# A searched schedule re-drawn, and three more buffers for the last output tiles: pooled attention into a gated conv FFN

## The chip, the cores and the metric

The kernel runs on one core of a Trainium2 chip. The metric is device time of one execution in microseconds, the median of three runs. Engines are called as in the profile: PE (TensorE matmul), PEld (its weight load), DVE (VectorE), ACT (ScalarE), POOL (GpSimd), SP (SyncE). POOL, SP and ACT issue DMAs.

## What is computed

Eight batches, eight heads, 576 positions, head size 64; all inputs and the output are float32.

```python
k_p = k.reshape(B, H, 72, 8, D).mean(axis=3)      # 72 pooled keys per head
v_p = v.reshape(B, H, 72, 8, D).mean(axis=3)
attn = softmax(scale * q @ k_p.T)                 # 576 x 72 for each head
x = (attn @ v_p), heads side by side              # (8, 576, 512)
h = maximum(x @ w_in, 0)                          # 512 -> 1024
conv_out = 3-tap convolution of h along the positions, conv_w per feature
out = (h * sigmoid(conv_out)) @ w_out             # 1024 -> 512, (8, 576, 512)
```

## The kernel before

**Tiles and stages.** Batches are taken in four groups of two. A group's attention runs in tiles of 128 rows of positions, nine to a group (ten in group 0). For a batch k, q and v are loaded (as bf16, by casting DMAs on POOL's queue; batch 0's k and q come as float32 over SP's queue into the two buffers `hT`, and are cast by ACT and DVE at L307). Keys are pooled on PE with a pooling matrix (L432, L442), or by adds on DVE (`pool_pair`, L465, group 1 on); the pooled keys are cast to `kT` (L457), queries are turned into `qT` (L542 on PE, copy at L560), values are pooled on DVE (L512, L516). An attention tile takes scores on PE (L608), the maximum on DVE (`negm`, L634), the exponential on ACT, a transpose with a copy `eT` (L707), the product with the values (L718), a reciprocal (L731), the scaling (L739 on ACT or L746 on DVE), and a turn of x into `xT` (for the early groups L763 on PE with the copy L771; later by DMA, L755).

**The FFN.** It runs by batch, in eight blocks of 128 features: `ffn_in` (L776, PE) and the relu (L785, ACT) into `hT`. The convolution of the early batches runs on PE (`ffn_conv`, L940). For batches 4 to 7 and half of batch 3 it runs on DVE, with two instructions a block (`ffn_tap`, L912), into one of three accumulators `tg`. Positions are laid out so that a tap is a shift by 64 columns; the first and last 64 columns need copies from the other end, and these are the **wraps**: `ffn_wrap` makes two small copies (L860, L861) for two feature blocks at a time, on POOL or on ACT. The outermost columns are zero, set once by `clear_ends` (four POOL memsets, L855 and L856). After the second tap ACT takes the sigmoid or tanh (L922) into `gT`, and DVE multiplies four blocks by h (`ffn_times`, L990). With all gates of a batch, or of both batches of the group for the tiles of the second, the output projection runs (`ffn_out`, L998, PE, eight matmuls a tile), then a copy to SBUF (`ffn_copy`, L1009, DVE or ACT) and two stores of 64 rows (L1021, queue of SP or ACT).

**Buffers.** `rings` (L218) says how many buffers of each kind there are. Output tiles use the ring `osb` (five), but the nine of group 3 use a ring of their own, `late`: eight halves of the four `qp` buffers, which held queries and are free by then.

**The order.** All instructions belong to ops that the builder puts into a graph. Nothing plans at run time: the class `Graph` holds tables that a search has written. An entry n of ORDER emits op n // 2 on engine n % 2 of those that it may run on; -1 emits a spare matmul (`fill`, L425) that keeps PE busy. FORMS says which matmul tiling an op takes where it may choose, PLACES which buffer of its ring each tile gets. Each engine then runs its own part of that list in order, waiting on semaphores for the others.

```python
for n in self.ORDER:
    o = spares.pop(0) if n < 0 else self.ops[n // 2]
    o.engine = list(o.engines)[0 if n < 0 else n % 2]
```

`clear_ends` is bound by one edge, `ends = add({"POOL": 0.8}, 0, clear_ends, after=raws)` (L1114): it comes after the casts of batch 0's raw keys and queries, which lie in the same buffers. POOL's loads share one DMA queue.

Of the kernel before, what the change touches and what calls it, by code (L numbers as in the profile page):

```python
# [33 lines left out]
class Graph:  # L34
# [38 lines left out]
        0, 16, 4, 24, 12, 44, 28, 8, 10, 14, 32, -1, -1, 42, 36, -1, -1, 40, -1, -1,  # L73
        2, -1, 38, -1, 66, 64, -1, -1, 19, 68, -1, 48, 21, -1, 60, -1, -1, 46, 102, 7,
        26, 34, 114, 118, 106, 116, 121, 108, 104, 113, 111, 122, 126, 125, 292, 128, -1, 74, 30, 294,
        358, -1, -1, 70, 360, 296, -1, -1, 298, 50, 362, 364, 336, 338, 58, 314, 300, 316, 340, -1,
        -1, 342, 130, -1, 318, -1, 344, 320, 132, 380, 303, 134, 322, 382, 347, 194, 196, 136, 384, 201,
        324, 72, 348, 386, 326, 199, 350, 366, 352, 78, 304, 369, 328, 206, 306, 330, 202, 209, 308, 370,
        204, 388, 354, 391, 372, -1, 548, 374, 310, 332, 550, 313, 392, 357, 394, 552, 396, 526, 554, 376,
        528, 398, 335, 570, 556, 401, 572, 530, 226, 532, 558, 574, 379, 228, 230, 576, 504, 444, 506, 84,  # L80
        233, 446, 62, 138, 508, 448, 482, 438, 510, 140, 440, 142, 426, 56, 442, 534, 428, 484, 432, 430,
        144, 434, 537, 52, 486, 76, 512, 488, 420, 436, 422, 514, 80, 560, 54, 424, 516, 402, 562, 518,
        564, 414, 416, 520, 404, 418, 466, 406, 210, 472, 470, 468, 212, 578, 566, 474, 408, 568, 476, 410,
        580, 478, 238, 412, 456, 241, 480, -1, 458, 450, 460, 214, 538, 452, 522, 540, 454, 542, 234, 525,
        462, -1, -1, 237, 582, 216, 262, 221, 584, 464, 82, 225, -1, -1, 219, -1, 223, -1, -1, 265,
        978, 586, 544, 490, 980, 547, 770, 588, 592, 982, 591, 493, 772, 748, 984, 594, 750, 600, 774, 597,
        752, 776, 258, 146, 494, 261, 602, 496, 148, 498, 1000, 605, 934, 608, 1002, 754, 150, 500, 1004, 778,
        503, 610, 936, 781, 756, 152, 613, 624, 759, 154, 626, 614, 86, 1006, -1, 938, 760, 642, 628, 156,
        90, 644, 940, 762, 158, 956, 764, 646, 1008, 942, 958, 94, 1011, 704, 630, 945, 706, 98, 632, 960,
        636, 22, 634, 638, 708, 672, 640, 160, 962, 242, 1012, 96, 676, -1, 782, 674, 986, 1014, 784, -1,  # L90
        88, 1016, 989, 792, 766, 794, 710, 654, 656, 786, 769, 1018, 796, 658, 964, 990, 967, 244, 946, 660,
        1021, 992, 948, 994, 662, 798, 968, 950, 664, 788, 800, 970, 791, 246, 678, 972, 803, 162, 248, 680,
        804, 682, 164, 92, 974, 255, 806, 666, 808, 257, 253, 668, 251, 166, 977, 810, 168, 1186, -1, 670,
        952, 1188, 100, 996, 813, -1, -1, 1190, 999, 694, 955, 170, 1204, 696, 1096, 1206, 1098, 698, 172, 726,
        1192, 1060, 1208, 1100, 1062, 728, 712, 1064, 648, 174, 730, 715, 650, 1090, 176, 652, 1092, 684, 732, 1168,
        688, 1094, 1170, 1104, 1072, 690, 1074, 178, 692, 270, 1076, 1172, 716, 273, 1066, 700, 1194, 1068, 1174, 616,
        1070, 718, 1176, 686, 618, 721, 1084, 180, -1, 702, 1086, 621, -1, 1088, 1150, 1140, 1152, 1210, 1078, 1118,
        1142, 1212, 1080, 1144, 1124, 266, 1082, 1154, 1054, 606, 269, 1102, 1056, 1120, 1196, 1058, 622, 734, 1126, 1428,
        737, 1222, 1198, 830, 1430, 1156, 290, 1224, 1201, 814, 1432, 816, 1226, 1128, 1178, 274, 738, 1122, 832, 819,
        740, 182, 722, 1180, 820, 838, 742, 725, 1182, 835, 744, 840, 1106, 747, 1184, 276, 1410, 843, 1134, 1412,  # L100
        1228, 1158, 884, 1136, 1108, 886, 1138, 1112, 1214, 1230, 888, 878, 1216, 1110, 1414, 880, 1446, 1218, 882, 872,
        1448, 874, 1434, 1220, 918, 278, 876, 1450, 890, 288, 922, 1146, 892, 920, 1160, 894, 846, 1162, 1114, 1165,
        860, 1148, 866, 1436, 868, 1116, 862, 184, 1166, 870, 848, 1130, 864, 280, 1132, 851, 1232, 1202, 283, 284,
        1234, 908, 287, 1236, 1676, 186, 1238, 910, 854, 912, 1678, 1438, 856, 1452, 1440, 836, 1680, 896, 858, 898,
        1442, 1416, 1454, 1640, 188, 902, 900, 1642, 1316, 190, 906, 1644, 1418, 1318, 904, 192, 1392, 1320, 924, 1394,
        1444, 1646, 1322, 1396, 928, 1324, 926, 914, 1280, 1326, 1456, 1398, 1282, 1334, 1458, 930, 1292, 1461, 1400, 1286,
        1288, 1382, 1294, 1648, 1284, 1304, 916, 1296, 1306, 1290, 1462, 1298, 1308, 932, 1300, 1328, 1682, 1402, 1310, 844,
        1302, 1404, 1384, 1312, 1407, 1330, 822, 1336, 1684, 824, 1342, 1314, 1408, 1338, 1604, 827, 1332, 1658, 1420, 1660,
        1340, 1046, 598, 1422, 1606, 1425, 1048, 1662, 1256, 1608, 1664, 1426, 1650, 1376, 1051, 1896, 1842, 1652, 1610, 1258,
        1898, 852, 1655, 1844, 1264, 1900, 1612, 1266, 1846, 1386, 1344, 1261, 1878, 1686, 1666, 1902, 1880, 1269, 1538, 1688,  # L110
        1882, 1848, 1540, 828, 1622, 1378, 1542, 1520, 1624, 1522, 1380, 1656, 1532, 1690, 1524, 1534, 1626, 1346, 1526, 1692,
        1348, 1528, 1536, 1860, 1364, 1530, 1550, 1614, 1262, 1022, 1628, 1616, 1350, 1619, 1548, 1668, 1630, 1862, 1030, 1670,
        1354, 1032, 1352, 1270, 1864, 1673, 1496, 1366, 1498, 1052, 1502, 1356, 1504, 1368, 1584, 1904, 1024, 1358, 1370, 1500,
        1508, 1586, 1674, 1510, 1506, 1632, 1027, 1372, 1544, 1514, 1866, 1634, 1516, 1620, 1360, 1374, 1038, 1590, 1518, 1040,
        1637, 1388, 1272, 1362, 1884, 1274, 1638, 1512, 1578, 1240, 1035, 1546, 1390, 1850, 1588, 1906, 1242, 1580, 1036, 1480,
        1592, 1043, 1482, 1277, 1908, 1596, 1868, 1582, 1746, 1910, 1594, 1748, 1598, 1044, 1752, 1750, 1754, 1570, 1600, 1734,
        1564, 1756, 1736, 1485, 1740, 1552, 1784, 1245, 1742, 1566, 1246, 1248, 1744, 1554, 1568, 1852, 1572, 1488, 1912, 1738,
        1854, 1782, 1602, 1574, 1758, 1760, 1886, 1556, 1870, 1558, 1857, 1250, 1028, 1802, 1490, 1560, 1762, 1764, 1858, 1872,
        1493, 1796, 1766, 1562, 1888, 1874, 1472, 1768, 1890, 1876, 1798, 1893, 1786, 1776, 1808, 1778, 1474, 1804, 1253, 1894,
        1464, 1576, 1477, 1806, 1770, 1478, 1810, 1800, 1772, 1466, 1816, 1774, 1494, 1780, 1988, 1790, 1812, 1946, 1818, 1486,  # L120
        1952, 1789, 1954, 1822, 1820, 1948, 1278, 1792, 1956, 1710, 1950, 1824, 1990, 1794, 1254, 1994, 1834, 1976, 1826, 1982,
        1828, 1469, 1978, 1836, 1992, 1712, 1980, 1830, 1984, 2008, 1970, 1832, 1718, 1814, 1838, 1964, 1986, 1966, 2010, 2001,
        1958, 1840, 1972, 1720, 1974, 2040, 1715, 1960, 2046, 1922, 1716, 1962, 2042, 1999, 1924, 2012, 1470, 2048, 1702, 2044,
        2002, 1968, 1726, 2028, 1997, 2050, 1704, 2004, 1927, 1938, 2030, 2006, 1928, 2014, 1940, 2032, 2034, 1728, 2020, 1930,
        1731, 2036, 1723, 1732, 1914, 2022, 2038, 1916, 2016, 2024, 2052, 1694, 2018, 1943, 1932, 1919, 2026, 1696, 1934, 2078,
        1699, 1937, 1700, 2054, 2056, 1707, 1944, 1921, 2080, 1708, 2070, 2082, 2058, 2062, 2085, 1724, 2072, 2061, 2064, 2074,
        2086, 2076, 2067, 2069, 2094, 2088, 2090, 2096, 2093, 2100, 2099,
    )
    FORMS = (
        1, 1, 1, 0, 0, 1, 1, 0, 0, 0, 1, 1, 0, 1, 1, 0, 0, 0, 1, 1, 1, 0, 1, 1, 1, 0, 0, 1, 0, 1, 0, 1, 1, 1, 1, 1, 1, 1, 0, 0,  # L130
    )
    PLACES = (
        1, 4, 1, 2, 0, 1, 2, 6, 0, 6, 2, 0, 5, 0, 6, 4, 6, 6, 2, 2, 0, 1, 1, 3, 0, 7, 4, 1, 1, 3, 1, 1, 2, 6, 0, 0, 0, 0, 0, 0,
# [50 lines left out]
def kernel(  # L184
# [43 lines left out]
    def banks(token):  # L228
# [20 lines left out]
        "sd": ([P, 2, 4, Sp], FP32),  # L249
    }  # L250
    buffers = {r: [const.tile(s, dt, name=f"{r}{i}") for i in range(rings[r])] for r, (s, dt) in shapes.items()}
    half_qp = [t.rearrange("p h s -> p (h s)")[:, i * 1024:(i + 1) * 1024] for t in buffers["qp"] for i in range(2)]
    buffers["late"] = [t.bitcast(FP32) for t in half_qp]
    tokens = {}

# [1244 lines left out]
```

## Time and profile before

| | us |
|---|---|
| median of 3 runs | 210.57 |
| lowest, highest | 210.29, 210.69 |
| profiled execution, its time | 210.06 |
| its span, first to last instruction | 208.3 |
| mean granted TensorE clock | 0.993 |

The span is what the profile's rows are measured against; the remaining 1.8 us of the execution lie around it. A row of a group reads: line, engine, operation, output <- input by the program's names, shape, count, then busy time and mean ns of one instruction, then idle time of the engine just ahead of these instructions and what ended most of it. A row of the timeline reads: start, duration, engine, line, operation, shapes, and in brackets the idle time ahead of it with its releaser. Rows with SPq or ACTq are DMA issues on that engine's queue.

### The profile page before, as it was taken

Reading aid. Unit: us, or ns where it says so; the run is one execution under the profiler, and the core shown is the slowest. Engines: PE = TensorE matmul, PEld = TensorE weight load, DVE = VectorE, ACT = ScalarE, POOL = GpSimd, SP = SyncE. Lnnn points to the kernel's source line nnn. Section 1 sums busy time; section 2 is a strip of 40 time slices with the busy share of each in tenths; the row PEclk is TensorE's granted clock in tenths of the full one; section 3 lists DMA queues with packets and bytes.
Section 4 is the critical chain, followed back from the end, with each engine's and each line's share of the span. In section 5 each row is a group of like instructions: output and inputs, shape, how many; then the busy total and the mean of one; then the engine's idle time right before and its main releaser. Section 6 shows DMA issues by size and latency. Waiting matters only on the chain.

```text
span 208.3 us, 6540 instructions
## 1 busy us (share of the span) xinstructions
PE 197.2 (95%) x2650; PEld 134.3 (64%) x2666; DVE 190.4 (91%) x338; ACT 174.5 (84%) x363; POOL 45.5 (22%) x74
## 2 busy tenths in 40 slices
PE   4999999999999999999999999999999999999990
PEld 2568688776688887666868875566556666644450
DVE  7979999889999999999999999999999999999440
ACT  3558786998899999998998999999999999797310
POOL 8553035010173211010000152040234315000000
PEclk9999999999999999999999999999999999999997
DMA  6999999999999999998497465565665557044395
GB/s 205 243 204 209 205 207 208 208 209 203 189 167 202 205 207 206 170 162 164 92 144 123 97 136 111 119 138 127 129 139 116 120 124 179 3 101 102 92 282 185
DMA packets 48835, 33.48 MB, mean 161 GB/s; under 512 B 28300, under 2 KB 43812, under 8 KB 48804
## 3 DMA queue, kind: packets, MB, share of 16 engines
q0 software_dynamic: 15216, 15.40, 45.1%
q1 hardware_dynamic: 32592, 16.20, 36.4%
q10 hardware_dynamic: 996, 1.45, 2.6%
q8 instruction: 21, 0.34, 0.6%
q14 instruction: 10, 0.08, 0.1%
HBM read 32.52 MB, written 9.44 MB: 201 GB/s over the span
## 4 chain that ended last, share of the span: by engine, by line
PE 49%; DVE 24%; ACT 16%; issue 5%; DMA 3%; SPq 0%; DVEq 0%; ACTq 0%
PE psum L776 19%; PE psum L998 13%; DVE tg L912 6%; DVE negm L634 4%; ACT x L739 4%; PE psum L718 3%; DVE gT L990 3%; DVE sd L646 3%; DMA hT<-in_k_dram 3%; PE psum L940 2%; ACT hT L785 2%; PE psum L693 2%; PE psum L608 2%; ACT gT L922 2%; ACT qT L560 2%
## 5 line engine op out<-in xcount | busy, mean ns | idle before, releaser
L776 PE MATMUL psum<-xT,w_in_sb 128*128 128x288 bf16 x512 | 70.6, 286 | 0.4
L998 PE MATMUL psum<-w_out_sb,gT 128*128 128x512 bf16 (+1 forms) x280 | 65.9, 373 | 1.1 <-issue 0.2
L776 PEld LDWEIGHTS <-w_in_sb 128*128 128x128 bf16 x512 | 48.4, 98 | 15.6 <-issue 0.6
L785 ACT ACTIVATE hT<-psum 128x576 bf16<-128x576 f32 x64 | 41.6, 671 | 4.8 <-PE psum L776 4.2
L998 PEld LDWEIGHTS <-gT 128*128 128x128 bf16 x296 | 27.7, 98 | 27.5 <-DVE gT L990 0.6
L860 POOL COPY hT<-hT 128x126 bf16<-128x126 bf16 x14 | 11.3, 810 | 84.2 <-issue 43.6
L912 DVE SCALAR_TENSOR_TENSOR tg<-hT,ratio 128x576 f32<-128x576 bf16 x36 | 28.2, 813 | 0.5 <-ACT gT L922 0.2
L634 DVE TENSOR_REDUCE negm<-psum 128x8 f32<-128x576 f32 (+2 forms) x37 | 27.4, 748 | 1.3 <-PE psum L608 0.6
L912 DVE SCALAR_TENSOR_TENSOR tg<-hT,ratio,tg 128x576 f32<-128x576 bf16 x36 | 28.2, 810 | 0.0
L922 ACT ACTIVATE gT<-tg,ratio 128x576 bf16<-128x576 f32 x36 | 27.4, 793 | 0.8 <-DVE tg L912 0.7
L990 DVE TENSOR_TENSOR gT<-gT,hT 128x2304 bf16<-128x2304 bf16 x16 | 21.4, 1348 | 0.1
L739 ACT ACTIVATE x<-psum,r 128x64 bf16<-128x64 f32 x96 | 21.2, 356 | 0.1
L1009 ACT COPY osb<-psum 128x512 f32<-128x512 f32 x27 | 16.4, 620 | 4.3 <-PE psum L998 2.7
L646 DVE TENSOR_TENSOR sd<-psum,negm 128x576 f32<-128x576 f32 x27 | 19.8, 747 | 0.1
L683 ACT ACTIVATE e<-sd 128x576 bf16<-128x576 f32 x27 | 19.4, 719 | 0.1
L718 PE MATMUL psum<-vm,eT 128*128 128x65 bf16 (+5 forms) x240 | 18.8, 222 | 0.2 <-DVE vm L516 0.2
L718 PEld LDWEIGHTS <-eT 128*128 128x128 bf16 (+1 forms) x240 | 14.8, 101 | 3.6 <-issue 0.8
L746 DVE TENSOR_TENSOR x<-psum,r 128x512 bf16<-128x512 f32 (+1 forms) x25 | 16.6, 679 | 0.2
L425 PE MATMUL psum<-gT 128*128 128x448 bf16 x40 | 12.7, 425 | 2.8 <-DVE gT L1107 2.8
L940 PE MATMUL psum<-hT,dw 64*64 64x63 bf16 (+2 forms) x448 | 13.2, 255 | 0.2 <-ACT kT L505 0.2
L512 DVE TENSOR_TENSOR v<-v 128x1280 bf16<-128x1280 bf16 (+2 forms) x24 | 12.9, 539 | 0.2
L940 PEld LDWEIGHTS <-dw 64*64 64x64 bf16 x448 | 10.9, 107 | 2.1 <-issue 1.5
(94 smaller groups left out, 236.5 us busy)
## 6 DMA issues: line engine op xcount, KB each, us to landing
out_dram<-osb SPq DMA_DIRECT2D x54, 128.0 KB, 2.4
v<-in_v_dram POOLq DMA_DIRECT2D x8, 512.0 KB, 13.7
qp<-in_q_dram POOLq DMA_DIRECT2D x7, 576.0 KB, 13.2
kk<-in_k_dram POOLq DMA_DIRECT2D x3, 1152.0 KB, 14.4
out_dram<-qp ACTq DMA_DIRECT2D x10, 128.0 KB, 3.4
hT<-in_k_dram SPq DMA_DIRECT2D x2, 576.0 KB, 5.0
w_in_sb<-in_moe_w_in_dram POOLq DMA_DIRECT2D x2, 512.0 KB, 15.4
w_out_sb<-in_moe_w_out_dram POOLq DMA_DIRECT2D x1, 1024.0 KB, 18.6
```

The lines of the kernel that those rows point to most:

```text
L634: nc.vector.tensor_reduce(out=a["m"][0:rows], in_=a["s"][0:rows, :, 0:2 * KW].rearrange("p a (h s) -> p a h s", s=Sp), axis=AX.X, op=OP.ma ...
L646: nc.vector.tensor_tensor(out=a["d"][0:rows], in0=a["s"][0:rows, :, 0:2 * KW].rearrange("p a (h s) -> p a h s", s=Sp), in1=a["m"][0:rows]. ...
L683: nc.scalar.activation(out=dst, in_=src, func=ACT.Exp,)
L718: nc.tensor.matmul(out=a["o"][lo:hi, h // 4, (h % 4) * (D + 1):(h % 4 + x1 - x0) * (D + 1)], lhsT=a["eT"][:, j, lo:hi], rhs=buf("vm", b)[: ...
L739: nc.scalar.activation(out=a["x"][0:rows, n * D:(n + 1) * D], in_=ov[:, n // 4, n % 4, 0:D], func=ACT.Identity, scale=r[0:rows, n // 4, n ...
L776: nc.tensor.matmul(out=banks(ps)[:, j, 0:SC], lhsT=w_in_block(dc, fb), rhs=buf("xT", g)[:, dc, i * S + j * SC:i * S + (j + 1) * SC], start ...
L785: nc.scalar.activation(out=h_of(b)[:, fb].rearrange("p (a s) -> p a s", a=2), in_=banks(ps)[:, :, 0:SC], func=ACT.Relu, scale=1.0 if (b, f ...
L912: nc.vector.scalar_tensor_tensor(out=acc, in0=h, scalar=w, in1=acc if tap else mid, op0=OP.mult, op1=OP.add)
L922: nc.scalar.activation(out=gate, in_=acc_of(b, fb, ps), func=squash(b, fb), scale=ratio[:, 1, fb:fb + 1])
L940: nc.tensor.matmul(out=banks(pss[r ^ c])[c * D:(c + 1) * D, j, lo:hi], lhsT=dw[r * D:(r + 1) * D, tap * n_fb + fb, :], rhs=hT[r * D:(r + 1 ...
L990: nc.vector.tensor_tensor(out=gate, in0=gate, in1=h_of(b)[:, four], op=OP.mult)
L998: nc.tensor.matmul(out=bank(ps)[0:rows, columns], lhsT=buf("gT", g)[:, fb, t * P:t * P + rows], rhs=w_out_sb[:, fb, columns], start=(fb == 0),
```

## The change

Four edits. The tables ORDER, FORMS and PLACES are replaced as a whole. The ring `late` grows from 8 to 11, its three new members being one part of each of the three v buffers, and a copy into a late tile then also follows the last reader of the values of batches 4 to 7.

```diff
     ORDER = (
-        0, 16, 4, 24, 12, 44, 28, 8, 10, 14, 32, -1, -1, 42, 36, -1, -1, 40, -1, -1,
...
+        0, 16, 4, 24, 8, 12, 44, 10, 14, 32, -1, -1, 42, 38, -1, 46, -1, 40, -1, 48,
...
-             "hT": 2, "gT": 2, "xT": 2, "qT": 3, "kk": 1, "qp": 4, "v": 3, "vm": 5, "kT": 5, "sd": 3, "r": 3, "s": 2, "late": 8}
+             "hT": 2, "gT": 2, "xT": 2, "qT": 3, "kk": 1, "qp": 4, "v": 3, "vm": 5, "kT": 5, "sd": 3, "r": 3, "s": 2, "late": 11}
...
     half_qp = [t.rearrange("p h s -> p (h s)")[:, i * 1024:(i + 1) * 1024] for t in buffers["qp"] for i in range(2)]
+    half_qp += [t.rearrange("p j x -> p (j x)")[:, 0:1024] for t in buffers["v"]]
...
-            osb, free = (token("late", g, t), [x for n in range(4, B) for x in qdone[n, 0]]) if g == 3 else (token("osb", g, t), [])
+            osb, free = (token("late", g, t), [x for n in range(4, B) for x in qdone[n, 0] + [vdone[n]]]) if g == 3 else (token("osb", g, t), [])
```

The added line shifts the numbers of all lines below L252 by one. The ops are the same in both kernels, with 40 spare matmuls in each. What the new tables do is seen in the engines' lists. Names with a number are buffers: `qp_74` to `qp_77` are the four query buffers, `osb_123` to `osb_127` the output ring, `v_87` to `v_89` the values, `tg_118` to `tg_120` the accumulators of the taps.

**POOL at its start**, from the second load of batch 0's queries (`qp_75`, four heads by 320 columns) on. Before:

```order
L285 DMA qp_75<-in_q_dram 128x4x320
L318 DMA v_88<-in_v_dram 128x4x512
L321 DMA v_88<-in_v_dram 64x512
L285 DMA kk_78<-in_k_dram 128x4x576
L285 DMA qp_74<-in_q_dram 128x4x576
L328 DMA w_in_sb_68<-in_moe_w_in_dram 128x4x512
L285 DMA qp_75<-in_q_dram 128x4x576
L318 DMA v_87<-in_v_dram 128x4x512
L321 DMA v_87<-in_v_dram 64x512
L328 DMA w_in_sb_67<-in_moe_w_in_dram 128x4x512
L292 DMA kk_78<-in_k_dram 128x9x512
```

and now:

```order
L286 DMA qp_75<-in_q_dram 128x4x320
L319 DMA v_88<-in_v_dram 128x4x512
L322 DMA v_88<-in_v_dram 64x512
L856 MEMSET hT_116 128x8
L857 MEMSET hT_116 128x8
L856 MEMSET hT_117 128x8
L857 MEMSET hT_117 128x8
L286 DMA kk_78<-in_k_dram 128x4x576
L286 DMA qp_74<-in_q_dram 128x4x576
L286 DMA qp_77<-in_q_dram 128x4x576
L329 DMA w_in_sb_68<-in_moe_w_in_dram 128x4x512
L329 DMA w_in_sb_67<-in_moe_w_in_dram 128x4x512
```

The four memsets of `clear_ends`, which stood some 60 us later, now stand ahead of batch 1's keys (`kk_78` 128x4x576), and so ahead of every load that follows. Batch 1's values (`v_87` before, `v_88` now) fall behind the second half of w_in, and batch 2's queries go to another buffer.

**DVE where group 1's keys are pooled** (the first row is the first of the three adds, L465, then L466), with the rows around it. Before:

```order
L465 TENSOR_TENSOR kk_78<-kk_78 128x9x256
L465 TENSOR_TENSOR kk_78<-kk_78 128x9x128
L771 COPY xT_114<-psum 128x4x128
L707 COPY eT_105<-psum 128x5x64
L980 TENSOR_SCALAR gT_121<-gT_121 128x2x576
L982 TENSOR_SCALAR gT_121<-tg_118 64x2x576 x2
L990 TENSOR_TENSOR gT_121<-gT_121,hT_117 128x4x576
L465 TENSOR_TENSOR kk_78<-kk_78 128x9x64
L731 RECIPROCAL r_111<-psum 128x8
L746 TENSOR_TENSOR x_109<-psum,r_111 128x512
```

and now:

```order
L466 TENSOR_TENSOR kk_78<-kk_78 128x9x256
L466 TENSOR_TENSOR kk_78<-kk_78 128x9x128
L732 RECIPROCAL r_111<-psum 128x8
L466 TENSOR_TENSOR kk_78<-kk_78 128x9x64
L747 TENSOR_TENSOR x_110<-psum,r_111 128x512
L981 TENSOR_SCALAR gT_121<-gT_121 128x2x576
L983 TENSOR_SCALAR gT_121<-tg_120 64x2x576 x2
L991 TENSOR_TENSOR gT_121<-gT_121,hT_116 128x4x576
L732 RECIPROCAL r_112<-psum 64x8
L747 TENSOR_TENSOR x_108<-psum,r_112 64x512
```

The copy of x into `xT`, which stood directly behind the second add, now stands some twenty rows ahead of the first; the copy of the `eT` tile left DVE. A reciprocal of an attention tile stands there instead.

**ACT on the last batch**, from just ahead of its seventh relu (L785, then L786) to behind its eighth (batch 7's h is in `hT_117` before, in `hT_116` now). Before:

```order
L785 ACTIVATE hT_117<-psum 128x576
L860 COPY hT_117<-hT_117 128x2x63
L861 COPY hT_117<-hT_117 128x2x63
L922 ACTIVATE gT_122<-tg_118,ratio 128x576
L922 ACTIVATE gT_122<-tg_119,ratio 128x576
L785 ACTIVATE hT_117<-psum 128x576
L860 COPY hT_117<-hT_117 128x2x63
L861 COPY hT_117<-hT_117 128x2x63
L922 ACTIVATE gT_122<-tg_120,ratio 128x576
```

and now:

```order
L923 ACTIVATE gT_122<-tg_118,ratio 128x576
L786 ACTIVATE hT_116<-psum 128x576
L923 ACTIVATE gT_122<-tg_119,ratio 128x576
L1010 COPY osb_124<-psum 128x512
L1010 COPY osb_125<-psum 128x512
L786 ACTIVATE hT_116<-psum 128x576
L923 ACTIVATE gT_122<-tg_120,ratio 128x576
L923 ACTIVATE gT_122<-tg_118,ratio 128x576
L923 ACTIVATE gT_122<-tg_119,ratio 128x576
```

The wraps of batch 7 are gone from ACT. POOL, which made one pair of these copies for batch 7, now makes all four pairs, as the last rows of its list. One of batch 6's wraps goes the other way. Of the last output tiles, one copy passes from ACT to DVE and one tile's pair of stores from ACT to SP. All late tiles are placed in halves of `qp` buffers, in both kernels.

## What I expect

> **What bounds the kernel now.** I read the busy times first, then a table by stretches, then the chain that ended last, then single rows of the timeline. The page's first part gives the shares:
>
> ```profile
> PE 197.2 (95%) x2650; PEld 134.3 (64%) x2666; DVE 190.4 (91%) x338; ACT 174.5 (84%) x363; POOL 45.5 (22%) x74
> ```
>
> PE stands highest, but some of that is filling: the costliest groups hold 40 spare matmuls that write a scrap bank when PE has nothing else to do.
>
> ```profile
> L425 PE MATMUL psum<-gT 128*128 128x448 bf16 x40 | 12.7, 425 | 2.8 <-DVE gT L1107 2.8
> ```
>
> So PE can give up to 12.7 us before it is the bound. The table by stretches cuts the span where the limits change; each row is start:end, length, then the busy time of each engine with its count, granted clock, DMA share and GB/s.
>
> ```profile
> 0.00:10.00 10.00, 6.91 (x67) 3.62 (x67) 8.36 (x34) 4.36 (x6) 7.31 (x17) 1.00 0.88 225
> 10.00:20.00 10.00, 9.54 (x229) 7.15 (x226) 8.28 (x19) 6.91 (x13) 4.58 (x6) 1.00 1.22 205
> 20.00:35.87 15.87, 15.60 (x258) 12.55 (x253) 14.74 (x32) 11.71 (x20) 4.25 (x6) 1.00 1.24 207
> 35.87:49.00 13.13, 12.87 (x313) 9.58 (x313) 11.80 (x20) 12.63 (x23) 1.03 (x1) 1.00 1.23 207
> 49.00:100.00 51.00, 50.50 (x847) 36.94 (x849) 50.38 (x90) 48.21 (x95) 9.93 (x20) 1.00 1.12 186
> 100.00:150.00 50.00, 49.25 (x641) 34.12 (x646) 49.62 (x84) 48.52 (x126) 8.28 (x14) 1.00 0.64 123
> 150.00:194.20 44.20, 43.70 (x270) 25.75 (x273) 43.79 (x59) 40.48 (x83) 10.08 (x10) 1.00 0.48 106
> 194.20:208.40 14.20, 8.83 (x48) 4.62 (x48) 3.40 (x6) 1.72 (x3) 0.00 (x0) 0.90 0.69 205
> ```
>
> The third busy figure is DVE. From 49 us to 194.2 us it is busy for 50.38 + 49.62 + 43.79 = 143.79 us of 145.2: only 1.41 us are idle in that long middle. From 35.87 to 49 us 1.33 us are idle, ahead of that 1.13, 1.72 and 1.64 us. The DVE therefore sets the pace up to 194 us, and the DMA share above 1.2 says that the loads set it in the first 49 us. Behind the DVE's last instructions hangs the end, as the chain shows:
>
> ```profile
> 182.80 8.83 DVE tg L912 x12
> 191.63 2.55 DVE gT L990 x2
> 194.23 8.84 PE psum L998 x48
> ```
>
> The last twelve taps, the last two products and the 48 matmuls of six output tiles follow each other without a gap. Three quantities set the time: when the first loads let the DVE go, the DVE's work from there to 194 us, and the tail.
>
> **The loads anchor the DVE.** The pair load of keys for group 1 goes through POOL's queue. The timeline shows where it is issued (start, duration), and what DVE starts with it:
>
> ```profile
> 17.99 1.02 POOL L292 DMA_DIRECT2D kk<-in_k_dram  x1 [3.91 <-ACT kT L457]
> 35.87 2.15 DVE L465 TENSOR_TENSOR kk<-kk 128x2304 bf16<-128x2304 bf16 x2
> ```
>
> The DMA part of that window has it landing 17.9 us after its issue, at 17.99 + 17.9 = 35.89 us:
>
> ```profile
> kk<-in_k_dram POOLq DMA_DIRECT2D x1, 1152.0 KB, 17.9
> ```
>
> The DVE starts to pool these keys at that very moment. Whatever it saves ahead of 35.87 us it would spend waiting for this transfer, as long as the queue delivers at the same time.
>
> **Part 1: the copies that change engine, −0.1 us.** The order lists show that ahead of the last product the DVE loses one cast of a 64x144 key block, one 128x512 query copy and one 128x320 copy, and gains one 64x288 cast. Their rows (busy and mean in ns behind the bar):
>
> ```profile
> L457 DVE CAST kT<-psum 64x144 bf16<-64x144 f32 x2 | 0.6, 300 | 0.0
> L560 DVE COPY qT<-psum 128x512 bf16<-128x512 bf16 x1 | 0.4, 425 | 0.0
> L707 DVE COPY eT<-psum 128x320 bf16<-128x320 bf16 x1 | 0.3, 315 | 0.0
> L457 ACT CAST kT<-psum 64x288 bf16<-64x288 f32 x2 | 0.8, 387 | 0.2 <-PE psum L442 0.2
> ```
>
> For the gained cast only ACT's 0.387 us exists, which I take for the DVE. That is 0.30 + 0.43 + 0.32 − 0.39 = 0.65 us less. All of it but some 0.1 us stands ahead of the anchor, so I count −0.1; the other end is −0.65, if the anchor doesn't hold. ACT takes these copies over; it is idle for 15.87 − 11.71 = 4.16 us of the third stretch, and costs nothing while that cover lasts.
>
> **Part 2: POOL's queue, +0.3 us.** The four memsets that clear the ends of the two h buffers (0.3 us in all) move from about 60 us to ahead of batch 1's key load. These buffers hold batch 0's raw keys and queries until they are cast, so POOL now stands still until the last cast is done, with every later load queued behind it:
>
> ```profile
> 5.22 0.71 POOL L321 DMA_DIRECT2D v<-in_v_dram  x1
> 5.92 0.78 POOL L285 DMA_DIRECT2D kk<-in_k_dram  x1
> 8.17 1.15 ACT L307 CAST kk<-hT 128x1152 bf16<-128x1152 f32 x1 [0.95 <-DMA hT<-in_k_dram]
> ```
>
> The cast ends at 9.32 us; with the memsets the issue goes from 5.92 to about 9.7 us. The load lands today at 5.92 + 10.4 = 16.32 us, because it queues behind two others. Its landing row, and three rows of loads that were less queued:
>
> ```profile
> kk<-in_k_dram POOLq DMA_DIRECT2D x1, 576.0 KB, 10.4
> qp<-in_q_dram POOLq DMA_DIRECT2D x1, 320.0 KB, 6.2
> v<-in_v_dram POOLq DMA_DIRECT2D x1, 512.0 KB, 6.9
> v<-in_v_dram POOLq DMA_DIRECT2D x1, 64.0 KB, 7.4
> ```
>
> Issued at 9.7 us it would land at 15.9, 16.6 or 17.1 us by these three, so between no loss and +0.8 us. I take the second, the nearest in size: +0.3. The queue is served one load after another, so the delay would reach the anchor undiminished. In the same queue batch 1's values fall behind a weight load; DVE's work on them falls back as well, ahead of the anchor, so I add nothing.
>
> **Part 3: batch 7's wraps from ACT to POOL, +0.2 us.** A wrap is two small copies, which the taps of its two blocks wait for. Of batch 7's four wraps three move to POOL; one of batch 6 goes the other way. By form:
>
> ```profile
> L860 POOL COPY hT<-hT 128x126 bf16<-128x126 bf16 x14 | 11.3, 810 | 84.2 <-issue 43.6 <-ACT hT L785 38.3 <-DVE r L731 1.4
> L860 ACT COPY hT<-hT 128x126 bf16<-128x126 bf16 x4 | 1.2, 294 | 0.1
> ```
>
> And the one time that today's trace shows taps waiting for a POOL wrap:
>
> ```profile
> 174.11 3.19 POOL L860 COPY hT<-hT 128x126 bf16<-128x126 bf16 x1 [6.86 <-issue]
> 177.25 0.29 POOL L861 COPY hT<-hT 128x126 bf16<-128x126 bf16 x1
> 177.34 0.82 DVE L912 SCALAR_TENSOR_TENSOR tg<-hT,ratio 128x576 f32<-128x576 bf16 x1 [0.19 <-POOL hT L860]
> ```
>
> The copy took 3.19 us, four times its mean, while four taps ran back to back, and the DVE then lost 0.19 us. Three wraps in the same position lose between nothing, where other taps cover them, and 3 x 0.29 = 0.87 us, one copy laid bare each. I take one waiting as above: +0.2. The Trainium skill, page "SBUF — State Buffer", section "Who interferes with whom", has a rule against this move: a DVE instruction with two SBUF inputs contends with a GpSimd instruction that reads SBUF, and whichever is first has the shared port to itself. The 3.19 us row agrees. By that rule each wrap waits until the taps in flight end, as in rival C.
>
> ACT, which gives the wraps up, has slack here: 44.2 − 40.48 = 3.7 us idle.
>
> **Part 4: the tail, −0.2 us.** The same 48 matmuls remain. One tile's copy and one tile's store pass from ACT to other engines (DVE copies, SP stores). The last rows today:
>
> ```profile
> 202.81 2.56 ACTq L1021 DMA_DIRECT2D out_dram<-qp  x4
> 201.96 2.46 SPq L1021 DMA_DIRECT2D out_dram<-qp  x4
> 196.31 5.84 ACTq L1021 DMA_DIRECT2D out_dram<-qp  x6
> 195.98 1.56 SPq L1021 DMA_DIRECT2D out_dram<-qp  x2
> ```
>
> ACT's queue is done last, at 205.37 us, SP's at 204.42. With a tile less on ACT, the end may fall back to SP's (−0.95), or SP with one more pair of 1.56 us may reach 205.98 (+0.61). The middle is −0.17, taken as −0.2. The copies that the DVE gains lie behind its last product, and it is idle there for 14.2 − 3.4 = 10.8 us.
>
> **Parts without a price.** The eleven late slots are never used beyond eight: by the order lists no late tile goes into a v buffer, and waiting for v's readers is met long before. Other places in the middle are permuted within some fifteen positions, with the same instructions; there DVE is idle for 1.41 us of 145, so nothing more can be won than that, and I count 0.
>
> **Sum.** −0.1 + 0.3 + 0.2 − 0.2 = +0.2 us. The profiled execution took 210.06 us (span 208.3), 0.51 below the median of 210.57. So 210.26 in a profile like it, 210.8 as a median. This kernel's runs lie within 0.2% of each other, and 0.2% (0.42 us) is about what a measurement can tell from no change: 210.15 to 210.99. My forecast's own range is 210.4 to 211.2.
>
> **Rivals.** *A, faster: the waits behind the anchor go.* The DVE waits twice in the fourth stretch:
>
> ```profile
> 38.63 0.43 DVE L771 COPY xT<-psum 128x512 bf16<-128x512 bf16 x1 [0.61 <-PE psum L763]
> 42.85 0.21 DVE L731 RECIPROCAL r<-psum 128x8 f32<-128x8 f32 x1 [0.50 <-PE psum L718]
> ```
>
> The copy that waited 0.61 us now stands ahead of the pooling, whose wait covers it. If the second wait goes too, 1.11 us are saved: 209.7. Against it: another operation now stands directly behind the pooling, waiting for the same PE. If the 0.65 us of part 1 are kept in full as well, 209.1.
>
> *B, slower: POOL's queue runs dry.* Batch 1's keys land at 17.1 instead of 16.6 us, and nothing behind catches up: +0.5, 211.3. It decides from the point at which the loads ahead of them are through before the new ones start; for it speaks that the value load ahead lands at 5.22 + 7.4 = 12.6 us, 2.9 us after the new issue, less time than any load quoted took; against it that the row nearest in size gives 16.6 us.
>
> *C, slower: the taps of batch 7 wait for POOL.* All three wraps are laid bare, +0.87 instead of +0.2: 211.5. For it speaks the 3.19 us row, against it that four other taps stand ahead of two of the three.
>
> *D: the change does not do what it says.* For the v buffers this is certain by the order lists; it changes no time.
>
> **Chances.** My forecast 0.36 (of it 0.03 faster, 0.24 the same, 0.09 slower), A 0.29 (0.28 faster, 0.01 the same), B 0.20 (0.19 slower, 0.01 the same), C 0.15 (0.14 slower, 0.01 the same). Faster 0.31, the same 0.27, slower 0.42. The range goes from A with all of part 1, 209.1, to B with the tail's upper end, 211.3 + 0.8 = 212.1; it also holds B and C together, 212.0.
>
> **What would show it.** Part 2: the issue of batch 1's keys near 9.7 us and the pooling of group 1's keys at 36.2 us (B: 36.7 or later; A with part 1: before 35.9). Part 3: waits for POOL ahead of taps behind 174 us, 0.2 us in sum (C: 0.9). Part 4: last stores done 11.0 us after the last product, now 205.37 − 194.18. Part 1: DVE's total, less its new tail copies, 0.65 us lower. I would be wrong in the base of the argument if DVE had over 2 us more or less idle time between 49 and 194 us: then the order of the middle decides, which I put at 0.

## The result, and the profile after

| | before | changed |
|---|---|---|
| median, us | 210.49 (4 runs) | 211.81 (4 runs) |
| lowest, highest | 210.29, 210.69 | 211.46, 212.04 |
| profiled execution, its span | 210.06, 208.3 | 212.04, 210.3 |

The ratio is 1.0061, with a 95% interval of 1.0041 to 1.0082: slower by 1.3 us, where 210.8 was forecast in a range of 209.1 to 212.1. The two profiled executions lie 1.98 us apart, more than the medians, so what is read from this pair of traces is somewhat too large.

The table by stretches of the changed kernel, in the same columns (the third busy figure is DVE):

```profile
0.00:10.00 10.00, 6.42 (x63) 3.65 (x64) 7.49 (x32) 5.07 (x8) 5.32 (x19) 1.00 0.87 217
10.00:20.00 10.00, 9.74 (x202) 6.47 (x203) 8.65 (x20) 5.58 (x12) 5.82 (x8) 1.00 1.21 202
20.00:35.87 15.87, 15.87 (x292) 12.34 (x289) 13.44 (x29) 13.26 (x22) 4.16 (x7) 1.00 1.24 207
35.87:49.00 13.13, 12.62 (x300) 9.55 (x299) 12.67 (x22) 11.88 (x21) 1.95 (x3) 1.00 1.23 207
49.00:100.00 51.00, 50.25 (x831) 37.03 (x833) 50.45 (x90) 48.68 (x97) 9.87 (x16) 1.00 1.12 181
100.00:150.00 50.00, 48.93 (x657) 34.10 (x660) 49.22 (x83) 47.95 (x124) 7.21 (x14) 1.00 0.64 124
150.00:194.20 44.20, 43.81 (x273) 25.98 (x276) 43.85 (x60) 40.28 (x81) 11.96 (x14) 1.00 0.55 117
```

Ahead of 35.87 us the DVE is idle for 2.51 + 1.35 + 2.43 = 6.29 us instead of 4.49; from there to 49 us for 0.46 instead of 1.33; behind 49 us little changes (0.55, 0.78 and 0.35 against 0.62, 0.38 and 0.41). What the DVE met ahead of pooling group 1's keys, and its last products:

```profile
27.75 0.76 DVE L635 TENSOR_REDUCE negm<-psum 128x8 bf16<-128x576 f32 x1 [0.84 <-PE psum L622]
...
30.95 0.83 DVE L513 TENSOR_TENSOR v<-v 128x1280 bf16<-128x1280 bf16 x1 [0.69 <-DMA v<-in_v_dram]
...
35.27 0.21 DVE L732 RECIPROCAL r<-psum 128x8 f32<-128x8 f32 x1 [0.51 <-PE psum L719]
...
36.96 2.14 DVE L466 TENSOR_TENSOR kk<-kk 128x2304 bf16<-128x2304 bf16 x2
...
192.50 2.62 DVE L991 TENSOR_TENSOR gT<-gT,hT 128x2304 bf16<-128x2304 bf16 x2
```

Between 27 and 36 us the DVE waits for scores from PE (0.84 us), for the values of batch 1 (0.69) and for products from PE (0.51); the rows of the kernel before show no wait between 24 and 38 us. The pooling starts at 36.96 instead of 35.87 us (+1.09), with no wait directly ahead of it, and the last product ends at 195.12 instead of 194.17 (+0.95). One row of the table by stretches for what lies between, first of the kernel before, then of the changed one:

```profile
35.87:194.17 158.30, 156.32 (x2064) 106.39 (x2078) 155.56 (x250) 149.81 (x323) 29.32 (x45) 1.00 0.80 145
```

```profile
36.96:195.12 158.16, 155.18 (x2038) 105.97 (x2041) 156.06 (x250) 148.37 (x318) 30.07 (x45) 1.00 0.81 146
```

The DVE is busy for 0.50 us more, and its idle time falls from 2.74 to 2.10 us. The two counts of 250 don't stand for the same instructions: behind the pooling the changed kernel has a 128x640 `eT` copy where the kernel before has a 128x320 one and the `xT` copy, and its count includes a scaling of x that runs 0.08 us into the stretch. So 1.09 + 0.50 − 0.64 = 0.95 us are there before the tail begins. How much of this is scatter, the experiments' traces tell. Four kernels have exactly the changed kernel's instructions up to the last product (changed, e1, e2, e5). In them the pooling starts at 36.91 to 37.54 us, against 35.87 to 36.15 us in the three with the head of the kernel before (before, e6, e9): that is clear. From the pooling to the last product the four take 157.93 to 158.79 us, so the −0.14 us of this stretch is not; the DVE is busy in it for 156.06 to 156.25 us in all four, so the 0.50 us comes again. The tail, from the last product to the end of the span, grew from 208.3 − 194.17 = 14.13 to 210.3 − 195.12 = 15.18 us: +1.05. Its rows on PE, ACT (with its queue) and DVE, and two rows of ACT in the kernel before:

```profile
195.18 8.83 PE L999 MATMUL psum<-w_out_sb,gT 128*128 128x512 bf16 x47 [0.33 <-DVE gT L991]
```

```profile
198.70 5.20 ACTq L1022 DMA_DIRECT2D out_dram<-qp  x6
204.02 0.58 ACT L1010 COPY qp<-psum 128x512 f32<-128x512 f32 x1 [10.16 <-PE psum L999]
204.64 2.70 ACTq L1022 DMA_DIRECT2D out_dram<-qp  x4
```

```profile
197.98 0.69 DVE L1010 COPY qp<-psum 128x512 f32<-128x512 f32 x1 [1.06 <-PE psum L999]
...
203.57 0.90 DVE L1010 COPY qp<-psum 128x256 f32<-128x256 f32 x2 [2.31 <-DMA out_dram<-qp]
```

```profile
194.80 1.36 ACTq L1021 DMA_DIRECT2D out_dram<-qp  x2
...
202.19 0.59 ACT L1009 COPY qp<-psum 128x512 f32<-128x512 f32 x1 [5.32 <-PE psum L998]
```

PE takes its 8.83 us as before and ends at 204.01. But ACT copies tile 5 only at 204.02, where it copied it at 202.19, 0.86 us ahead of PE's end (184.68 + 18.37 = 203.05 in the row of experiment 3), in the kernel before; and its last stores follow that copy. ACT's queue starts to issue at 198.70 instead of 194.80, because the first store in its list is that of tile 7, which DVE copies from 197.98 on.

### The profile page after: what moved, and what is told of

Its sections match the earlier page's. It is cut to its first block, busy times and chain, and to the rows that moved or that the text cites. A ratio compares the mean times of both kernels' runs of the same rounds, so it can differ in the third digit from the quotient of the medians.

```text
span 210.3 us, 6540 instructions
## 1 busy us (share of the span) xinstructions
PE 197.1 (94%) x2650; PEld 133.8 (64%) x2666; DVE 191.4 (91%) x338; ACT 173.3 (82%) x359; POOL 46.3 (22%) x78
## 4 chain that ended last, share of the span: by engine, by line
PE 64%; DVE 12%; ACT 10%; DMA 7%; issue 3%; SPq 1%; ACTq 0%; DVEq 0%
PE psum L777 22%; PE psum L999 20%; PE psum L719 5%; PE psum L941 4%; DMA hT<-in_k_dram 3%; DMA xT<-x 2%; PE psum L426 2%; PE psum L694 2%; DMA out_dram<-osb 2%; DVE negm L635 2%; DVE gT L991 2%; DVE sd L647 2%; PE psum L764 2%; ACT hT L786 2%; ACT osb L1010 2%
## 5 line engine op out<-in xcount | busy, mean ns | idle before, releaser
L777 PEld LDWEIGHTS <-w_in_sb 128*128 128x128 bf16 x512 | 47.9, 98 | 16.0 <-issue 1.0
L786 ACT ACTIVATE hT<-psum 128x576 bf16<-128x576 f32 x64 | 41.1, 671 | 3.1 <-PE psum L777 2.6
L684 ACT ACTIVATE e<-sd 128x576 bf16<-128x576 f32 x27 | 18.9, 703 | 0.1
L1010 ACT COPY osb<-psum 128x512 f32<-128x512 f32 x26 | 15.4, 612 | 1.2 <-PE psum L999 1.1
L561 ACT COPY qT<-psum 128x1152 bf16<-128x1152 bf16 (+2 forms) x11 | 10.8, 989 | 2.4 <-PE psum L543 1.6
```

Of the source, the lines that this page charges most:

```text
L777: nc.tensor.matmul(out=banks(ps)[:, j, 0:SC], lhsT=w_in_block(dc, fb), rhs=buf("xT", g)[:, dc, i * S + j * SC:i * S + (j + 1) * SC], start ...
L786: nc.scalar.activation(out=h_of(b)[:, fb].rearrange("p (a s) -> p a s", a=2), in_=banks(ps)[:, :, 0:SC], func=ACT.Relu, scale=1.0 if (b, f ...
L1010: copy(out=osb[0:rows, columns], in_=bank(ps)[0:rows, columns])
```

## The experiments

Ratios are to the kernel before, on the same chip. All kernels start from the changed one; where an edit moves an op, tiles that no longer fit their PSUM bank or buffer get another.

**The tail.** Two causes offer themselves for tile 5's late copy: its half of a `qp` buffer is still being stored for tile 7 (the three v buffers are not used), or ACT is still issuing the three stores ahead of it.

*1. e1_free_slots: no half is used twice.* The last row of PLACES:

```diff
-        2, 4, 0, 0, 2, 2, 5, 7, 0, 0, 1,
+        2, 4, 0, 0, 2, 2, 5, 7, 8, 0, 9,
```

> The changed kernel with two entries of PLACES changed: output tile 5 of batch 7 goes to a half of a v buffer (slot 8) and tile 8 to another (slot 9), so no late slot is used twice and both copies lose their wait for a store to land. Theory 1 (reuse): in the changed kernel tile 5's copy started at 204.03 us though its matmuls ended at 202.48, because the store of tile 7 out of the same half had to land first; without that wait the copy starts near 202.5, and the end comes 1.0 to 1.5 us earlier (ratio to the kernel before 0.999 to 1.002). Theory 2 (ACT's queue): the copy stood behind tile 6's store on ACT, which was issued until 203.91; then the copy stays at about 204.0, only tile 8's first copy moves by some 0.2 us, and the time gains 0 to 0.2 us (ratio 1.005 to 1.007).

Measured: 212.27 us, 1.0088 (1.0057 to 1.0120). No gain, and more than either theory had. ACT's rows:

```profile
199.28 4.98 ACTq L1022 DMA_DIRECT2D out_dram<-qp  x6
204.36 0.58 ACT L1010 COPY v<-psum 128x512 f32<-128x512 f32 x1 [9.91 <-DVE v L1010]
```

Tile 5 now goes to a v buffer, and its copy still starts where the six issues end (204.26); the DVE copy that the bracket names was done at 204.17. Reuse alone isn't the cause.

*2. e2_store_order: tile 1's store ahead of tile 7's on ACT.*

```diff
+        1929,
         2085, 1936, 2056, 2074,
-        1929,
```

> The changed kernel with one store moved: on ACT, tile 1's store now stands ahead of tile 7's, as its copy was done at 196.92 us and tile 7's only at 198.67. All buffers as in the changed kernel. Theory 2 (ACT's queue): ACT starts to issue at 197.0 instead of 198.7, is through with tile 6's store some 1.2 us earlier, tile 5's copy starts near 202.7, and the end comes 0.7 to 1.3 us earlier (ratio 1.000 to 1.003). Theory 1 (reuse): tile 7's store can't go earlier, it lands when it did, tile 5's copy stays at about 204.0, and the time is that of the changed kernel (ratio 1.005 to 1.007).

Measured: 211.69 us, 1.0053 (1.0032 to 1.0075). ACT's rows:

```profile
196.79 5.50 ACTq L1022 DMA_DIRECT2D out_dram<-qp  x6
203.79 0.59 ACT L1010 COPY qp<-psum 128x512 f32<-128x512 f32 x1 [10.08 <-DMA out_dram<-qp]
```

The issues end at 202.29, and the copy still starts at 203.79: now it waits for a store to land, as the releaser says. The first run speaks against reuse, the second against the queue, and both theories are too simple: each cause stands right behind the other.

*3. e5_tail_both: both edits.*

> Both edits of the first two runs in one kernel: late tiles 5 and 8 of batch 7 in v buffers, and tile 1's store ahead of tile 7's on ACT. Theory of two causes in line (ACT's queue ends at the same moment as tile 7's store lands, so taking either away alone shows the other): tile 5's copy now starts within 0.3 us of the end of its matmuls, 0.8 to 1.0 us ahead of PE's last matmul instead of at it, and the span ends 5.0 to 5.3 us behind PE's last matmul, as in the kernel before (5.2), instead of 6.0 to 6.3; 0.8 to 1.0 us less, ratio 1.000 to 1.003. Rival (SP's queue sets the end, whatever ACT does): tile 5's copy moves, but the end stays 5.8 us or more behind PE's last matmul, ratio 1.004 to 1.006.

Measured: 211.37 us (12 runs), 1.0040 (1.0022 to 1.0058): past the theory's 1.003, at the lower end of the rival's 1.004 to 1.006. The profile is of the slowest of the twelve, 212.40 us. PE's and ACT's rows of this kernel, and PE's of the kernel before:

```profile
196.03 8.83 PE L999 MATMUL psum<-w_out_sb,gT 128*128 128x512 bf16 x47 [0.33 <-DVE gT L991]
```

```profile
197.81 5.69 ACTq L1022 DMA_DIRECT2D out_dram<-qp  x6
203.60 0.59 ACT L1010 COPY v<-psum 128x512 f32<-128x512 f32 x1 [8.88 <-DMA out_dram<-qp]
204.61 3.18 ACTq L1022 DMA_DIRECT2D out_dram<-v  x4
```

```profile
184.68 18.37 PE L998 MATMUL psum<-w_out_sb,gT 128*128 128x512 bf16 x90
```

The copy starts right behind the six issues (203.50), 1.26 us ahead of PE's end (204.86). The span ends 210.6 − 204.86 = 5.7 us behind PE's end; that is a little over the 5.0 to 5.3 expected, so I compare all kernels of the study, which differ in other places but have one of these tails:

| tail | span's end behind PE's last matmul, us | mean |
|---|---|---|
| of the kernel before: before, e7, e8, e10 | 5.25, 5.46, 5.4, 5.8 | 5.5 |
| changed: changed, e3, e4, e6, e11 | 6.3, 6.0, 6.1, 6.2, 6.2 | 6.2 |
| one edit: e1, e2 | 6.1, 6.05 | 6.1 |
| both edits: e5, e9, e12 | 5.7, 5.2, 5.8 | 5.6 |

By these means the changed tail costs about 0.7 us; either edit alone, in one kernel each, gives next to nothing back, and both nearly all of it. That the median fell by 0.44 us from the changed kernel's fits, but the intervals overlap.

**The head.** What makes the pooling late?

*4. e3_ends_back: the memsets behind the loads again.*

```diff
         121, 108,
-        22,
         106, 105,
...
         958, 1008, 96,
+        22,
```

> The changed kernel with the four memsets of clear_ends moved back behind the loads of the first 60 us; all else as changed. Theory of POOL's queue: batch 1's keys are issued near 5.8 us and land by 16.4 instead of 16.96, group 1's keys land at 35.9 instead of 36.44, and the pooling on DVE, which stood at 36.96 us, starts about 0.5 us earlier; the last product ends 0.3 to 0.6 us earlier (ratio 1.003 to 1.005). Rival (the order of DVE's and PE's work ahead of the pooling): DVE's waits for PE (0.84 and 0.51 us between 27 and 36 us) and for batch 1's values (0.69 us) stay, the pooling stays at 36.7 us or later, and the time gains 0 to 0.2 us (ratio 1.005 to 1.007).

Measured: 212.16 us, 1.0076 (1.0049 to 1.0103). The DVE's rows:

```profile
30.38 0.83 DVE L513 TENSOR_TENSOR v<-v 128x1280 bf16<-128x1280 bf16 x1
31.50 0.76 DVE L635 TENSOR_REDUCE negm<-psum 128x8 bf16<-128x576 f32 x1 [0.29 <-PE psum L609]
...
35.35 0.21 DVE L732 RECIPROCAL r<-psum 128x8 f32<-128x8 f32 x1 [0.78 <-PE psum L719]
...
37.04 2.14 DVE L466 TENSOR_TENSOR kk<-kk 128x2304 bf16<-128x2304 bf16 x2
```

The wait for the values of batch 1 is gone; the waits for PE grew by 0.29 + 0.27 us, the 0.84 us for scores stayed, and so did the pooling. POOL's rows say why little else moved:

```profile
17.99 0.74 POOL L319 DMA_DIRECT2D v<-in_v_dram  x1 [8.32 <-DVE vm L517]
...
19.25 1.03 POOL L293 DMA_DIRECT2D kk<-in_k_dram  x1
```

Batch 1's keys are issued at 5.77 instead of 9.86 us, but land at 5.77 + 11.0 = 16.8 instead of 16.96. Batch 1's values go into the buffer of batch 0's in the changed kernel, so POOL waits until those are read, and the pair load behind them is issued no earlier; it lands at 19.25 + 17.0 = 36.25 instead of 36.44, where the theory had 35.9. The rival holds for the pooling: moving the memsets back gains nothing here. The run doesn't take the late landing of the pair load away.

*5. e11_head_both: the memsets back, and four spare matmuls fewer between 19 and 25 us.*

```diff
-        72, -1, 366,
+        72, 366,
...
-        370, -1, 372,
+        370, 372,
...
-        357, -1, 550,
+        357, 550,
...
-        528, -1, 379,
+        528, 379,
```

> The changed kernel with clear_ends back behind the loads (as in e3) and without the four spare matmuls that it places between 19 and 25 us, where its PE has no idle time (15.87 of 15.87 us busy from 20 to 35.87). Theory (in the changed head two waits end together: the late values of batch 1, through POOL's queue, and a PE that is full, so that e3 alone showed nothing): DVE pools group 1's keys at 36.0 to 36.4 instead of 37.0 us, the last product ends 0.5 to 0.8 us earlier than in the changed kernel, ratio 1.002 to 1.004. Rival (PE only waits elsewhere when the spare matmuls go): the pooling stays at 36.9 or later, ratio 1.005 to 1.008.

Measured: 212.23 us, 1.0071 (1.0056 to 1.0086), the pooling at 37.01 us. The rival again: these four spare matmuls aren't what holds PE. The wait for scores stays too (0.88 us).

*6. e4_v1_early: batch 1's values ahead of the second half of w_in, in a buffer of their own.*

```diff
         336, -1,
+        70,
         58, 338,
...
         196, 346,
-        70,
         322, 198,
```

> The changed kernel with batch 1's values loaded ahead of the second half of w_in, as in the kernel before, and into a v buffer of their own, so that POOL doesn't wait for batch 0's values to be read. Theory of the late values: they land near 27.7 us instead of 30.8, DVE's wait of 0.69 us at 30.95 goes, the pooling of group 1's keys starts at 36.4 us, now at their landing, and the last product ends some 0.4 us earlier (ratio 1.004). Rival: the second half of w_in, now 2.7 us later, holds PE, and the time stays or grows by up to 0.5 us (ratio 1.006 to 1.009).

Measured: 214.04 us, 1.0174 (1.0144 to 1.0204), well past the rival's 1.006 to 1.009. The DVE then waits for PE where it had waited for the values:

```profile
32.95 0.76 DVE L635 TENSOR_REDUCE negm<-psum 128x8 bf16<-128x576 f32 x1 [2.22 <-PE psum L609]
...
38.49 2.14 DVE L466 TENSOR_TENSOR kk<-kk 128x2304 bf16<-128x2304 bf16 x2
```

In the changed order PE takes a block with the second half of w_in ahead of these scores, and that half now came later:

```profile
30.32 1.16 PE L777 MATMUL psum<-xT,w_in_sb 128*128 128x288 bf16 x8 [1.60 <-DMA w_in_sb<-in_moe_w_in_dram]
```

The loads and PE's order are tied to each other.

*7. e12_mended: all of it together.* To the edits of e2, e1, e3 and e4 come two on PE: the block that needs w_in's second half trades places with one that doesn't (420, 422, 424 with 432, 434, 436), and the products with the values of two attention tiles, on which the DVE's work ahead of the pooling depends, go ahead of that block:

```diff
+        516, 560, 418,
         420, 422,
...
-        418,
...
-        516, 560,
```

> The changed kernel with the suspected causes of both ends mended together. Head: clear_ends back behind the loads, batch 1's values loaded ahead of the second half of w_in into a buffer of their own, PE's blocks 3 and 5 of batch 0 exchanged (so that no block needs the second half of w_in before 32 us, which held PE in e4), and the products with the values of tiles 6 and 8 ahead of block 3, since the pooling of group 1's keys stands behind them on DVE. Tail: both edits of e5. Theory (the values of batch 1 come late, and with them the pooling): the pooling starts at 36.0 to 36.5 us instead of 37.0, the last product ends at 194.3 to 194.8, the end comes 5.2 to 5.7 us behind PE's last matmul; ratio 0.999 to 1.003. Rival (the head's loss is not in that chain, the last product follows from the middle): the pooling moves, but the last product ends at 195.0 us or later; ratio 1.003 to 1.006.

Measured: 214.35 us, 1.0180 (1.0163 to 1.0198). The DVE's rows:

```profile
36.57 2.14 DVE L466 TENSOR_TENSOR kk<-kk 128x2304 bf16<-128x2304 bf16 x2
40.39 0.21 DVE L732 RECIPROCAL r<-psum 128x8 f32<-128x8 f32 x1 [1.68 <-PE psum L719]
```

The pooling moved forward by 0.39 us, less than the theory had. This kernel moves the loads and PE's order together, so the run doesn't tell which of them did it. The DVE then waits 1.68 us for PE directly behind the pooling and is idle for 2.77 instead of 0.46 us from 35.87 to 49 us, and the last product ends at 197.73: nothing of the gain arrives. The rival had the late product, but not this time; with waits of its own the kernel doesn't show that the rival's reason is right.

**Crosses of the two tables.** One kernel's order up to some op, the other's from there.

*8. e6_before_head, e7_after_head, e8_before_end.* The edit is the whole table ORDER: its first 266 ops from one kernel and the rest from the other (e8: the first 953). Engines, forms and buffers follow; the joins also change the number of spare matmuls, to 41 in e6, 39 in e7 and 42 in e9.

> A cross of the two tables: the first 266 ops stand as in the kernel before (up to about 48 us), the rest in the order of the changed kernel; engines, forms and buffers follow the half that an op is in. Theory (the head's loss lies in the order of work in the first 49 us): the last product ends near 194.4 instead of 195.1 us, 0.5 to 0.8 us earlier than in the changed kernel, with the changed tail kept: ratio 1.002 to 1.004. Rival (the loss lies in the middle, between 49 and 194 us): the last product ends at 195.0 or later, ratio 1.005 to 1.008.

> The opposite cross: the first 266 ops as in the changed kernel, the rest in the order of the kernel before, with its tail. Theory (loss in the first 49 us): the last product ends near 194.9 instead of 194.2 us, and with the old tail the time is 0.5 to 0.8 us above the kernel before: ratio 1.002 to 1.004. Rival (loss in the middle): the last product ends by 194.4, ratio 0.999 to 1.001.

> The first 953 ops as in the changed kernel, the rest, from about 180 us on, in the order of the kernel before, with its late slots and its queues for the stores. Theory (the changed order of the last copies and stores costs 0.8 to 1.1 us): the span ends 5.2 us behind PE's last matmul and the time is 0.8 to 1.1 us below the changed kernel: ratio 1.001 to 1.003. Rival (the last stores only wait for what comes late from the middle): no gain beyond 0.3 us, ratio 1.005 to 1.007.

Measured: 213.79 us, 1.0144 (1.0118 to 1.0169); 214.48, 1.0182 (1.0158 to 1.0206); 216.58, 1.0273 (1.0243 to 1.0304). All three are slower than either kernel, which no theory had. Part of it I had put there: the join gave spare matmuls other banks, and they then waited. The third fill of e7 in its place, and of the changed kernel:

```profile
22.34 0.35 PE L426 MATMUL psum<-gT 128*128 128x448 bf16 x1 [0.52 <-ACT qT L561]
```

```profile
21.54 0.35 PE L426 MATMUL psum<-gT 128*128 128x448 bf16 x1
```

*9. e9_before_head_clean and e10_after_head_clean: the same with each fill in its own bank* (joins at op 260 and 240; e9 has both edits of the tail).

> The cross of e6 again, but with every spare matmul kept in its own bank (in e6 to e8 the join had put spare matmuls into other banks, where PE then waited for readers): the first 260 ops as in the kernel before, the rest as in the changed kernel, with both edits of the tail from e5. Theory (the head's loss lies in the first 49 us): the last product ends near 194.4 us instead of 195.1, the end comes 5.2 to 5.7 us behind PE's last matmul, and the time is within 0.3% of the kernel before: ratio 0.998 to 1.002. Rival (the loss lies in the changed middle): the last product ends at 195.0 or later, ratio 1.003 to 1.006.

> The opposite cross, spare matmuls in their own banks: the first 240 ops as in the changed kernel, the rest as in the kernel before, with its tail. Theory (loss in the first 49 us): last product near 194.9 us instead of 194.2, the end 5.2 us behind PE's last matmul, ratio 1.002 to 1.005. Rival (loss in the middle): last product by 194.4, ratio 0.999 to 1.001.

Measured: 213.14 us, 1.0124 (1.0100 to 1.0149), and 212.24, 1.0063 (1.0042 to 1.0084). The DVE's idle time in the stretches, with the start of the pooling (each figure is a stretch's length less the DVE's busy time in it):

| | 0 to 35.87 | pooling at | 35.87 to 49 | 49 to 194.2 |
|---|---|---|---|---|
| before | 4.49 | 35.87 | 1.33 | 1.41 |
| changed | 6.29 | 36.96 | 0.46 | 1.68 |
| e9, head of before | 4.49 | 36.14 | 2.53 | 1.84 |
| e10, head of changed | 6.28 | 37.04 | 1.73 | 1.53 |

The late pooling goes with the changed head, as the theory has it. But from 35.87 to 49 us both crosses are idle for longer than the kernel whose head they have, by 1.20 us (e9) and 1.27 us (e10). I read this as the price of the join, where neither order finds done what it counts on; no run separates it. The time of e9 lies beyond both theories, that of e10 just above what mine had, and the last products come at 196.84 and 195.30 us. So the crosses place the late pooling, and not the price of the head.

## Why the prediction went as it did

**The base** held: the DVE is idle for 0.55 + 0.78 + 0.35 = 1.68 us between 49 and 194.2 us, against 1.41, far from the 2 us that would have refuted it.

**Part 1 (−0.1)** is wrong by 0.6 us. The copies left as listed, though the gained cast took 0.449 us on DVE, not ACT's 0.387. But the DVE was busy for 0.50 us more behind the pooling instead of 0.1 less. Up to the last product it was busy for 0.25 us less (0.75 less ahead of the pooling), where I had 0.65. The rows that changed places don't explain it: behind the pooling two copies are gone (0.43 and 0.32 us, at 38.63 and 38.97 in the kernel before) and this one came in, 0.27 us less in sum:

```profile
46.46 0.48 DVE L708 COPY eT<-psum 128x640 bf16<-128x640 bf16 x1
```

What the rest is stays open. It comes again in e1, e2 and e5, with 156.06 to 156.25 us against the 155.56 of the one trace of the kernel before, and no run tried its cause.

**Part 2 (+0.3)** has the right transfer, and the wrong cause and consequence. Batch 1's keys were issued at 9.86 us and landed 7.1 us later at 16.96, in the bounds of 15.9 to 17.1; the pair load landed 17.4 us behind its issue, at 36.44, +0.55. The issues, and the landings by the DMA part of their windows:

```profile
9.86 0.77 POOL L286 DMA_DIRECT2D kk<-in_k_dram  x1 [0.31 <-issue]
...
17.78 0.75 POOL L319 DMA_DIRECT2D v<-in_v_dram  x1 [4.18 <-DVE vm L517]
...
19.04 1.04 POOL L293 DMA_DIRECT2D kk<-in_k_dram  x1
```

```profile
kk<-in_k_dram POOLq DMA_DIRECT2D x1, 576.0 KB, 7.1
kk<-in_k_dram POOLq DMA_DIRECT2D x1, 1152.0 KB, 17.4
```

The middle row is a wait that I had overlooked: for the buffer that batch 1's values now share with batch 0's. It, and not the memsets, stands ahead of the pair load; without the memsets (experiment 4) the pair load landed only 0.19 us earlier, and with them, but with a buffer of their own for these values (experiment 6), it was issued at 17.83 and landed at 17.83 + 18.1 = 35.9 us. The step that failed is "the delay would reach the anchor undiminished". The anchor had gone: DVE reached the pooling at 36.96, after the keys were there. I had seen in before that DVE and transfer met at 35.87 us and read it as the DVE waiting; by the row ahead of it, it had arrived at 34.49 + 1.24 = 35.73 us, so the transfer held it for 0.14 us and no more (0.33 us in e9, with the same head):

```profile
34.49 1.24 DVE L746 TENSOR_TENSOR x<-psum,r 128x512 bf16<-128x512 f32 x2
```

**The step that I priced at nothing** is part of where the head lost. "DVE's work on them falls back as well, ahead of the anchor, so I add nothing": the DVE waited for the values of batch 1 until 30.95 us, and PE has two blocks of the FFN (16 matmuls) ahead of the products with them:

```profile
33.23 0.66 DVE L517 TENSOR_TENSOR vm<-v,mask_wide 128x960 bf16<-128x960 bf16 x1
```

```profile
32.36 2.12 PE L777 MATMUL psum<-xT,w_in_sb 128*128 128x288 bf16 x16
...
34.65 0.87 PE L719 MATMUL psum<-vm,eT 128*128 128x130 bf16 x12
```

In the kernel before these products start at 33.38, ahead of the last 16:

```profile
33.38 0.87 PE L718 MATMUL psum<-vm,eT 128*128 128x130 bf16 x12
34.10 2.12 PE L776 MATMUL psum<-xT,w_in_sb 128*128 128x288 bf16 x16
```

DVE's scaling of these products stands ahead of the pooling. The longest of the three waits, 0.84 us for scores at 27.75, is not a wait for these values: it stays at 0.84 to 0.88 us in experiments 4 to 7, and no run takes it away. Shown: that the late pooling goes with the changed head, and which instructions DVE waits for in it. Not shown: how the head's loss divides among these waits, or one edit that gives it back; that stays open.

**Part 3 (+0.2)** came by its sign, and not as a cost. A wrap was held up once, for 0.19 us, as the taps' row tells:

```profile
176.75 2.52 POOL L861 COPY hT<-hT 128x126 bf16<-128x126 bf16 x1 [6.07 <-issue]
179.22 0.29 POOL L862 COPY hT<-hT 128x126 bf16<-128x126 bf16 x1
179.31 1.59 DVE L913 SCALAR_TENSOR_TENSOR tg<-hT,ratio 128x576 f32<-128x576 bf16 x2 [0.19 <-POOL hT L861]
```

The kernel before had lost the same 0.19 us, at 177.34 us, in the row that I priced the move from. So the move added nothing, and the term should have been 0. Rival C, 0.87 us, did not come: the copy of 2.52 us ran beneath two taps and a product that had to run anyway, and the DVE lost only the 0.19 us behind them. The Trainium skill's rule that a DVE instruction with two SBUF inputs and a GpSimd instruction that reads SBUF contend for the shared port ("SBUF — State Buffer", "Who interferes with whom") agrees with the 2.52 us of the copy.

**Part 4 (−0.2)** is the other failure: +0.7 us over all kernels, +1.05 in the profiled pair, outside my bounds of −0.95 to +0.61. The last store's issue ended 207.34 − 195.12 = 12.22 us behind the last product, where I had 11.0. I counted the stores of each queue and let them begin as before. The count is right, but ACT's first store belongs to a tile copied at 197.98, so the queue starts 3.9 us later and ends 2 us later, of which 0.95 us is the late product; and the halves reused by tiles 5 and 8 close the way around it. The bound should have been taken from when each store's copy is done.

**Rivals.** A came in its own stretch (0.46 instead of 1.33 us idle behind the anchor, 0.87 of the 1.11 us that I gave it) and was paid for ahead of it: waits moved from behind the pooling to ahead of it. D holds: no late tile lies in a v buffer. Using these buffers helps nothing by itself (experiment 1), and helps beside the other order of stores (experiment 3). The time went the way that I gave 0.42, but neither B nor C is why: 36.96 us is the sign that I gave for B, and the DVE wasn't waiting for keys.

That 211.81 us lies in my range is luck. Its upper end was made of B and of +0.61 for the tail; the pooling came late for another reason, the tail lost more, and 0.64 us less waiting behind the pooling stood against both in the profiled pair.

No kernel here beats the kernel before.

## What to carry to other kernels

Where two engines arrive together, undoing one cause shows nothing: twice here (reuse and queue in the tail, values and PE in the head) a single edit moved only the name behind the wait, and once (loads and PE's order) it made a longer one. So read the bracket after an edit, not only the time, and try the second edit on top before dropping the first. For stores behind a list of copies, a queue's end is counted from when its first entry can start, in the order of the queue, and not from how many entries it has.

## What the runs showed of the hardware that I had not expected

A spare matmul isn't free if it's put into a bank that is being read: in e7 such a fill waited 0.52 us for an ACT copy, and started at 22.34 instead of 21.54 us. Kernels with the same instructions up to the last product end that product between 194.96 (e2) and 195.98 us (e5); the raw keys' cast started at 8.27 and 8.70 us in these two, so some of it is there within the first 9 us. And the six issues on ACT's queue in the tail took 5.20 us, 0.87 each, and the copy behind them started at 204.02 us, 0.12 us after the last of them; the last copies of this kernel had better not stand behind stores on that engine.
